# Batch 0 of a fused attention and feed-forward kernel, laid out as 72 rows of eight tokens instead of 96 rows of six

## The chip, the cores and the metric

The kernel runs on one NeuronCore of a Trainium2 chip. Its time is the device time of one launch in microseconds (us), and lower is better. The core has five engines that run side by side and meet through semaphores: TensorE (PE, matrix products; PEld is its weight load), VectorE (DVE), ScalarE (ACT), GpSimd (POOL) and SyncE (SP), which here only issues DMAs. Sixteen DMA engines move data between HBM and the on-chip memory SBUF, which has 128 partitions; a tile of R rows lies in R partitions. PSUM is the small memory that TensorE writes its results into.

## What is computed

```python
# q, k, v: (8, 8, 576, 64)   p: (8, 8, 32, 64)    batch, heads, tokens, width
p_packed = sm_attn(p, k, v)               # softmax over the 576 tokens
out      = sm_attn(q, p_packed, p_packed) # softmax over the 32 packed rows
x = out.transpose(0, 2, 1, 3).reshape(8 * 576, 512)
h = x @ w_in                              # w_in: 512 x 2048, float64
g = h * tanh(softplus(h))                 # "mish"
return (g @ w_out).astype(float32)        # w_out: 2048 x 512, float64
```

## The kernel before

**Two kinds of work.** Nearly all of the time goes to the feed-forward products of the eight batches, 16 steps of 128 hidden columns per batch (`t` counts them over all batches). Each step does an "up" product into `ps_h`, `mish` on ACT, and a "down" product into four accumulators `acc`. The attention of batch b+1 is woven between the steps of batch b. Only the attention of batch 0 has nothing to hide behind: it is the opening, written out by hand line by line, and the engines SP, DVE, ACT and POOL follow that written order up to the end of batch 0. TensorE follows the written order throughout.

**The opening.** Heads are taken in two groups g = 0, 1 of four. `load_heads` fetches one group of k, q or v in two DMAs of two heads each, 288 KB a DMA, into tiles `[R, 2, NI, 2*D]`. With `SI = 6` tokens to a row there are `R = 96` rows, and one contiguous run of HBM is 6 x 64 x 4 = 1536 bytes; `NI = SI // 2 = 3`. The tiles k_t, q_t and v_t share one tag with `KVB = 8` buffers, so the loads of the second group of q and of v wait until TensorE has read k_t. The steps are, for each g:

- `turn_keys` and `turn`: 4 transposes for each of the `NI` slices, then one copy per slice from PSUM (`ps_kq`) to `kT` or `qT`, on the engines named in the call.
- `score`, `spread`, `sums`: the first scores, their exponentials into the tile `a1` (`a` in the profile), the sums.
- `turn_weights`: the exponentials are transposed into PSUM and copied to `a1T`.
- `values`: 4 x `SI` small products of `a1T` with `v_t`, summed over the `SI` tokens of a row in PSUM (`ps_pp`), then scaled into `pp`. `turn_values` transposes that into `ppT`.
- `match`, `peak`, `rise`, `tally`, `divide`, `back`: the second scores, which DVE transposes into `a2`, their softmax, and the result `at` that the feed-forward steps read. `a2` has the tag `"a"` with one buffer, which it shares with `a1`: DVE can only write `a2` when TensorE has read the last of `a1` in `turn_weights(1)`.
- `warm(n)`: n products on zeros, which keep TensorE running.

**The weights** arrive as float64 and are turned into float32 on the chip, in 32 pieces of 512 KB. `fetch(n)` issues the DMAs of the pieces up to n into `w_st` (`STB = 8` buffers), `words(n)` does the two ACT passes (L591, L592) and the two POOL passes (L593, L597) of the pieces up to n, and `join(n)` the two DVE passes (L603, L608). The pieces are here called w0, w1 and so on: w0, w1, w3, w4, w7, w8 are of w_in (2 KB runs), w2, w5, w6 of w_out (4 KB runs). `w_out` piece i is needed by the down product of step i. The loop calls `join(2t + 5)` and `words(2t + 9)` in the steps t up to 13, and `join(3)` in step 0.

**The DMA queue.** All loads go out on SP in written order. The tool that builds the program gives the DMAs eight semaphores in turn, so that a DMA is issued only after the eighth before it has landed.

**The end of batch 0.** `rows(c)` cuts the 128 rows of chunk c of the output into pieces that lie in one token position each, one DMA for each piece: eight DMAs in batch 0.

Of the kernel before, what the change touches and what calls it, by code (L numbers as in the profile page):

```python
# [8 lines left out]
F32 = mybir.dt.float32  # L9
F32R = mybir.dt.float32r  # L10
# [5 lines left out]

LAG = 2
GB = 3
KVB = 8
KQB = 5  # L20
STB = 8
WB = 4
# [17 lines left out]
def body(  # L40
# [12 lines left out]
    B, H, S, D = q.shape  # L53
    NP = p.shape[2]
    DF = w_in.shape[1]
    DO = w_out.shape[1]
    P = 128
    SI = 6
    R = S // SI
    NI = SI // 2  # L60
    NX = 9
# [10 lines left out]
    att = ctx.enter_context(tc.tile_pool(name="att", bufs=2))  # L72
    stat = ctx.enter_context(tc.tile_pool(name="stat", bufs=2))
    wts = ctx.enter_context(tc.tile_pool(name="wts", bufs=2))
    moe = ctx.enter_context(tc.tile_pool(name="moe", bufs=2))
    ps_acc = ctx.enter_context(tc.tile_pool(name="ps_acc", bufs=4, space=bass.MemoryType.PSUM))
    ps_h = ctx.enter_context(tc.tile_pool(name="ps_h", bufs=2, space=bass.MemoryType.PSUM))
    ps_a = ctx.enter_context(tc.tile_pool(name="ps_a", bufs=2, space=bass.MemoryType.PSUM))
# [40 lines left out]
    w_out_v = w_out.bitcast(I32).rearrange("(t p) m -> p t m", p=P)  # L119
    out_v = out.rearrange("(b p si) m -> b si p m", p=R, si=SI)  # L120

    def load_heads(src, b, g, tag):
        ts = []
        for h0 in (4 * g, 4 * g + 2):
            t = early.tile([R, 2, NI, 2 * D], F32, name=tag, tag="kvq", bufs=KVB)
            nc.sync.dma_start(
                out=t, in_=src[b, h0:h0 + 2].rearrange("h (p i x) d -> p h i (x d)", i=NI, x=2)
            )
            ts.append(t)
        return ts  # L130

    def of_slot(ts, g, h):


        return ts[h // 2][:, (h % 2) ^ g]

    def psum(pool, shape, name):
        return pool.tile(shape, F32, name=name, tag="acc" if pool is ps_acc else "ps_a")
# [31 lines left out]
    class Batch:  # L170
# [11 lines left out]

        def start(self, pool):
            self.ppT = moe.tile([P, 2, P], F32, name="ppT")
            self.aT_hi = moe.tile([P, 2, S], F32R, name="aT_hi")
            self.aT_lo = moe.tile([P, 2, S], F32R, name="aT_lo")
            self.qT, self.a1T, self.pp, self.floats = {}, {}, {}, {}
            self.pT = att.tile([P, 2, P], F32, name="pT", bufs=1)
            self.a1 = att.tile([P, 2, 2, NI, R], F32, name="a1", tag="a", bufs=1)
            self.rs = stat.tile([P, 2], F32, name="rs")  # L190
            ps = psum(pool, [P, 2, P], "ps_p")
            for g in range(2):
                nc.tensor.transpose(
                    out=ps[:, g, :], in_=self.p_t[:, g].rearrange("a u d -> a (u d)"), identity=ident
                )
            nc.vector.tensor_copy(out=self.pT[:, 0], in_=ps[:, 0])
            pairs = [x.rearrange("p (m t n) -> p m t n", t=2, n=NP) for x in (self.pT[:, 1], ps[:, 1])]
            for t in range(2):
                nc.vector.tensor_copy(out=pairs[0][:, :, t], in_=pairs[1][:, :, 1 - t])
# [40 lines left out]
        def values(self, g, pool):  # L240
            pp_ps = psum(pool, [P, D], "ps_pp")
            for n in range(SI):
                i, u = n // 2, n % 2
                for h in range(4):
# [3 lines left out]
                        rhs=of_slot(self.v_t[g], g, h)[:, i, u * D:(u + 1) * D],  # L248
                        start=(n == 0), stop=(n == SI - 1),
                        tile_position=(0, h * NP),  # L250
# [25 lines left out]
        def match(self, g, pool):  # L276

            s2 = scores(pool, self.ppT[:, g, :], self.qT[g])
            if g == 0:
                self.a2 = att.tile([P, 2, S // NP, NP], F32, name="a2", tag="a", bufs=1)  # L280
            a2f = self.a2[:, g].rearrange("a g n -> a (g n)")
            for u in range(2):
                nc.vector.transpose(out=a2f[:, u * HALF:(u + 1) * HALF], in_=s2[u])
            yield
# [78 lines left out]
        def rest_rows(self):  # L363
            return out_v[self.b, SI - 1, R - REST:R, :]

# [3 lines left out]
    class Later(Batch):  # L369
# [38 lines left out]

        def start(self):
            self.ppT = moe.tile([P, 2, P], F32, name="ppT")  # L410
            self.aT_hi = moe.tile([P, 2, S], F32R, name="aT_hi")
            self.aT_lo = moe.tile([P, 2, S], F32R, name="aT_lo")
            self.pp, self.floats = {}, {}
            self.pT = att.tile([P, 2, P], F32, name="pT", bufs=1)
            self.a1 = att.tile([P, 2, NX, NP, 2], F32, name="a1", tag="a", bufs=1)
            self.rs = stat.tile([P, 2], F32, name="rs")
            self.pinned(nc.vector.transpose(
                out=self.pT.rearrange("a g n -> a (g n)"), in_=self.p_t.rearrange("a h d -> a (h d)")
            ))
# [153 lines left out]
    class Weight:  # L573
# [6 lines left out]
        def fetch(self):  # L580
            self.st = stg.tile([P, 2 * FC], I32, name="w_st")
            nc.sync.dma_start(
                out=self.st.rearrange("p (m x) -> p m x", m=2),
                in_=w_in_v[:, 2 * self.g:2 * self.g + 2, self.n * FC:(self.n + 1) * FC],
            )
            self.dst = wi[self.n // 2][self.g][:, self.n % 2].rearrange("p m x -> p (m x)")

        def words(self):
            x = self.st.rearrange("p (n t) -> p n t", t=2)
            self.r = stg.tile([P, FC], I32, name="wround", bufs=WB)  # L590
            nc.scalar.activation(out=self.dst, in_=x[:, :, 1].bitcast(F32), func=AF.Copy, scale=F64_SCALE)  # L591
            nc.scalar.activation(out=self.r, in_=x[:, :, 0].bitcast(U32), func=AF.Copy, scale=2.0 ** -29)  # L592
            nc.gpsimd.tensor_scalar(  # L593
                out=self.dst, in0=self.dst, scalar1=F64_HIGH, scalar2=-F64_HIGH, op0=ALU.min, op1=ALU.max
            )
            self.sign = stg.tile([P, FC], F32, name="wsign", bufs=WB)
            nc.gpsimd.tensor_scalar(  # L597
                out=self.sign, in0=self.dst, scalar1=0.0, scalar2=1.0, op0=ALU.mult, op1=ALU.mult
            )

        def join(self):
            bits = self.dst.bitcast(I32)
            nc.vector.scalar_tensor_tensor(  # L603
                out=bits, in0=bits, scalar=3, in1=self.sign.bitcast(I32),
                op0=ALU.logical_shift_left, op1=ALU.bitwise_or,
            )
            yield
            nc.vector.tensor_tensor(out=bits, in0=bits, in1=self.r, op=ALU.add)  # L608
# [28 lines left out]
    def packed_floats(n, g):  # L637
        if g == 0:
            whole[n] = wts.tile([P, 2, QC], F32, name="wp_0", tag="wp_hi", bufs=4)
        ps = ps_a.tile([P, QC], F32, name=f"ps_w{g}", tag="ps_a")  # L640
        for h in range(4):
            weave(0, ps, wi[n // 2][g][:, n % 2, h // 2], g, h)
        nc.scalar.copy(out=whole[n][:, g], in_=ps)
        return whole[n]
# [144 lines left out]
    def together(*gens):  # L789
        gens = list(gens)  # L790
        while gens:
            gens = [x for x in gens if next(x, "end") != "end"]
# [30 lines left out]
    def warm(n):  # L823
        for _ in range(n):
            nc.tensor.matmul(out=ps_warm, lhsT=still, rhs=still, start=True, stop=True)  # L825
# [28 lines left out]
    with tc.manual_schedule(engines={mybir.EngineType.PE}):  # L854
        first = batches[0]
# [7 lines left out]
        first.k_t.append(load_heads(k, 0, 1, "k_t"))  # L863
        fetch(1)
        first.q_t = [load_heads(q, 0, 0, "q_t")]
        first.v_t = [load_heads(v, 0, 0, "v_t")]
        first.start(ps_a)
        first.turn_keys(0, ("ACT", "DVE", "ACT"))
        first.q_t.append(load_heads(q, 0, 1, "q_t"))
        fetch(2)  # L870
        warm(WARM[1])
        first.score(0)
        first.turn_keys(1, ("ACT", "DVE", "ACT"))
        first.spread(0)
        first.v_t.append(load_heads(v, 0, 1, "v_t"))
        fetch(STB)
        words(1)
        first.sums(0)
        warm(WARM[1])
        first.score(1)  # L880
        together(first.turn_weights(0, ps_acc, ("DVE", "ACT")))
        first.spread(1)
        together(first.turn(0, ps_acc, ("ACT", "ACT", "ACT")))
        join(1)
        first.sums(1)
        together(first.values(0, ps_a))
        warm(WARM[2])
        together(first.turn_values(0, ps_a))
        words(2)
        warm(WARM[2])  # L890
        together(first.match(0, ps_acc))
        together(first.turn_weights(1, ps_acc, ("ACT", "ACT")))
        first.peak(slice(0, 1))
        together(first.turn(1, ps_acc, ("ACT", "ACT", "ACT")))
        first.rise(slice(0, 1))
        together(first.values(1, ps_a))
        warm(WARM[2])
        join(2)
        together(first.turn_values(1, ps_a))
        first.tally(slice(0, 1))  # L900
        words(3)
        warm(WARM[2])
        together(first.match(1, ps_acc))
        first.peak(slice(1, 2))
        first.rise(slice(1, 2))
        first.divide(slice(0, 1))
        first.back(0)
        packed_floats(0, 0)
        wps = {(0, 0): packed_floats(0, 1)}
        words(4)  # L910
        nc.scalar.preload_act_table_set("mish")
        warm(WARM[3])
        first.tally(slice(1, 2))
        first.back(1, 2)
        words(5)
        groups = []
        gen = iter(())
        g_rest = None
# [120 lines left out]
```

## Time and profile before

| | us |
|---|---|
| median of 3 runs (lowest, highest) | 751.86 (750.21, 754.09) |
| the profiled execution's own time | 754.06 |
| its span in the profile | 752.1 |
| granted TensorE clock, mean | 0.997 |
| PE busy | 735.8 (98%) |
| DVE, ACT, POOL busy | 423.3, 298.3, 53.1 |

The profile shows one execution. A window view gives the busy time of each engine in a stretch of time, which for PE is close to the whole stretch except at the beginning. A timeline row has start, duration, engine, line, operation and tiles; in square brackets stands how long the engine was idle before it and what ended that. In the view of the DMA queues "us to landing" is the time from the issue of a DMA until all of it has arrived, and the share of a queue is the time that its packets took, out of the time of 16 engines.

### The profile page before, as it was taken

The page shows a single profiled execution, that of the slowest core. Times are in us where ns is not written, and L with a number is a line of the kernel's source. Part 1 is how long each engine was busy: PE and PEld are TensorE (multiplying, and loading weights), DVE is VectorE, ACT ScalarE, POOL GpSimd, SP SyncE. Part 2 cuts the span into 40 slices and gives each one's busy share as a digit, 9 for nine tenths or more (in the row PEclk, how much of TensorE's full clock was granted, in tenths as well). Part 3 has the DMA queues.
Part 4 walks back from the last instruction along what each step waited for, and adds up shares of the span by engine and source line. Part 5 has one row for each costly group of instructions (what it writes and reads, how often), then busy time and mean ns, then how long its engine had stood idle before and what let it go on. Part 6 is the DMA issues. An engine that isn't in the chain of part 4 may idle for free.

```text
span 752.1 us, 12729 instructions
## 1 busy us (share of the span) xinstructions
PE 735.8 (98%) x5162; PEld 565.4 (75%) x5162; DVE 423.3 (56%) x723; ACT 298.3 (40%) x696; POOL 53.1 (7%) x70
## 2 busy tenths in 40 slices
PE   9789999999999999999999999999999999999997
PEld 7545554678787888877788878877888777888886
DVE  3789767765846456464834547373753637332332
ACT  4675755453532524252522524243433424232221
POOL 1285440000000000000000000000000000000000
PEclk9999999999999999999999999999999999999999
DMA  9999970554204450143302442052201100010002
GB/s 229 286 283 228 297 131 1 118 80 88 39 1 103 67 99 1 56 72 64 64 1 71 71 96 32 10 111 40 57 1 42 29 2 1 1 57 1 0 1 71
DMA packets 186874, 56.40 MB, mean 75 GB/s; under 512 B 173760, under 2 KB 176064, under 8 KB 186816
## 3 DMA queue, kind: packets, MB, share of 16 engines
q1 hardware_dynamic: 186816, 55.59, 31.9%
q8 instruction: 41, 0.67, 0.4%
q14 instruction: 17, 0.14, 0.1%
HBM read 46.14 MB, written 9.44 MB: 74 GB/s over the span
## 4 chain that ended last, share of the span: by engine, by line
PE 91%; DVE 3%; ACT 3%; DMA 1%; issue 1%; POOL 0%; SPq 0%; POOLq 0%; ACTq 0%
PE ps_h L704 25%; PE acc L741 15%; PE acc L743 14%; PE acc L742 14%; PE acc L761 5%; PE ps_w L622 4%; PE ps_s L437 3%; PE ps_rest L743 2%; PE ps_rest L742 2%; PE ps_rest L741 2%; PE ps_pp L492 2%; DMA w_st<-in_moe_w_in_dram 1%; PE ps_warm L825 1%; PE ps_a L479 1%; PE ps_h L716 1%
## 5 line engine op out<-in xcount | busy, mean ns | idle before, releaser
L725 ACT ACTIVATE g<-ps_h 128x288 f32<-128x288 f32 (+1 forms) x256 | 97.8, 385 | 315.3 <-PE ps_h L704 282.8
L741 PE MATMUL acc<-wo_hi,g_hi 128*128 128x512 f32 x448 | 183.4, 409 | 0.0
L743 PE MATMUL acc<-wo_hi,g_lo 128*128 128x512 f32 x448 | 176.5, 394 | 0.0
L742 PE MATMUL acc<-wo_lo,g_hi 128*128 128x512 f32 x448 | 176.3, 394 | 0.0
L704 PE MATMUL ps_h<-aT_hi,wp_hi 128*128 128x288 f32 x496 | 157.5, 318 | 0.7 <-ACT g L725 0.7
L704 PE MATMUL ps_h<-aT_lo,wp_hi 128*128 128x288 f32 x496 | 146.1, 295 | 0.0
L704 PE MATMUL ps_h<-aT_hi,wp_lo 128*128 128x288 f32 x496 | 145.7, 294 | 0.0
L736 DVE CAST g_hi<-g 128x512 fp32r<-128x512 f32 x112 | 47.6, 425 | 163.2 <-ACT g L725 163.0
L741 PEld LDWEIGHTS acc<-wo_hi,g_hi 128*128 128x128 f32 x448 | 84.0, 187 | 43.2 <-issue 27.8
L704 PEld LDWEIGHTS ps_h<-aT_hi,wp_hi 128*128 128x128 f32 x496 | 93.1, 188 | 16.2 <-issue 3.8
L704 PEld LDWEIGHTS ps_h<-aT_lo,wp_hi 128*128 128x128 f32 x496 | 93.2, 188 | 14.7 <-issue 5.5
L743 PEld LDWEIGHTS acc<-wo_hi,g_lo 128*128 128x128 f32 x448 | 84.1, 188 | 19.7
L704 PEld LDWEIGHTS ps_h<-aT_hi,wp_lo 128*128 128x128 f32 x496 | 93.1, 188 | 0.0
L742 PEld LDWEIGHTS acc<-wo_lo,g_hi 128*128 128x128 f32 x448 | 84.3, 188 | 8.7
L737 DVE TENSOR_TENSOR g_lo<-g,g_hi 128x512 fp32r<-128x512 f32 x112 | 77.3, 690 | 5.8
L761 PE MATMUL acc<-wo,g 128*128 128x512 f32 x128 | 64.3, 606 | 3.3 <-DVE wo L608 1.6
L634 DVE TENSOR_TENSOR wp_lo<-ps_w,wp_hi 128x512 fp32r<-128x512 f32 x56 | 36.1, 684 | 16.7 <-ACT wp_hi L633 16.7
L633 ACT CAST wp_hi<-ps_w 128x512 fp32r<-128x512 f32 x56 | 30.1, 590 | 31.0 <-PE ps_w L622 31.0
L622 PE MATMUL ps_w<-wi,ppT 64*32 64x512 f32 (+1 forms) x576 | 38.1, 553 | 0.2 <-DVE wi L608 0.2
L761 PEld LDWEIGHTS acc<-wo,g 128*128 128x128 f32 x128 | 21.3, 189 | 21.8 <-issue 11.7
L727 ACT ACTIVATE g_rest<-ps_h 128x64 f32<-128x64 f32 x128 | 28.1, 220 | 0.0
L743 PE MATMUL ps_rest<-wo_hi,r_lo 128*128 128x512 f32 x64 | 25.1, 393 | 0.0
(113 smaller groups left out, 741.6 us busy)
## 6 DMA issues: line engine op xcount, KB each, us to landing
w_st<-in_moe_w_in_dram SPq DMA_DIRECT2D x16, 512.0 KB, 7.7
w_st<-in_moe_w_out_dram SPq DMA_DIRECT2D x16, 512.0 KB, 7.2
k_n<-in_k_dram SPq DMA_DIRECT2D x56, 144.0 KB, 3.2
q_n<-in_q_dram SPq DMA_DIRECT2D x56, 144.0 KB, 3.2
v_n<-in_v_dram SPq DMA_DIRECT2D x56, 128.0 KB, 2.7
out_dram<-o SPq DMA_DIRECT2D x28, 256.0 KB, 2.0
k_t<-in_k_dram SPq DMA_DIRECT2D x4, 288.0 KB, 4.3
q_t<-in_q_dram SPq DMA_DIRECT2D x4, 288.0 KB, 8.5
```

The lines of the kernel that those rows point to most:

```text
L622: nc.tensor.matmul(out=ps[h * NP:(h + 1) * NP, :], lhsT=ppTb[row:row + D, g, h * NP:(h + 1) * NP], rhs=w[row:row + D], start=True, stop=Tr ...
L633: nc.scalar.copy(out=hi, in_=ps)
L634: nc.vector.tensor_tensor(out=lo, in0=ps, in1=hi.bitcast(F32), op=ALU.subtract)
L704: nc.tensor.matmul(out=ps, lhsT=w[:, fs], rhs=a[:, g, cs], start=(n == 0), stop=(n == 5))
L725: nc.scalar.activation(out=self.act[:, hf * HALF:hf * HALF + m], in_=ps[:, :m], func=AF.Mish)
L727: nc.scalar.activation(out=self.g_rest[self.b % 2][self.f // 4][:, self.f % 4, :], in_=ps[:, m:], func=AF.Mish)
L736: nc.vector.tensor_copy(out=hi, in_=self.act)
L737: nc.vector.tensor_tensor(out=lo, in0=self.act, in1=hi.bitcast(F32), op=ALU.subtract)
L741: nc.tensor.matmul(out=acc, lhsT=hi[:, cs], rhs=wh, start=start, stop=False)
L742: nc.tensor.matmul(out=acc, lhsT=hi[:, cs], rhs=wl, start=False, stop=False)
L743: nc.tensor.matmul(out=acc, lhsT=lo[:, cs], rhs=wh, start=False, stop=stop)
L761: nc.tensor.matmul(out=accs[c], lhsT=grp.act[:, cs], rhs=wo[f], start=f == 0, stop=f == NF - 1)
```

## The change

Batch 0 is laid out with `SI = 8`, so `R = 72`, `NI = 4`, and a contiguous run is 2048 bytes; the tiles grow by a third per partition and `KVB` falls from 8 to 6, so that v waits for k's buffers. The loads and the weight steps are written in another order: w1 is fetched ahead of v, w2 and w3 ahead of the second group of v, and the ACT and DVE passes of several pieces move to earlier places. `a2` is put into a spare buffer of the tag of `aT_hi`.

```diff
-KVB = 8
+KVB = 6
-    SI = 6
+    SI = 8
-            self.aT_hi = moe.tile([P, 2, S], F32R, name="aT_hi")
+            self.aT_hi = moe.tile([P, 2, S], F32R, name="aT_hi", tag="aT_hi")
...
-                self.a2 = att.tile([P, 2, S // NP, NP], F32, name="a2", tag="a", bufs=1)
+                self.a2 = moe.tile([P, 2, S // NP, NP], F32, name="a2", tag="aT_hi")
...
         first.k_t.append(load_heads(k, 0, 1, "k_t"))
         fetch(1)
         first.q_t = [load_heads(q, 0, 0, "q_t")]
+        fetch(2)
+        first.start(ps_a)
+        first.turn_keys(0, ("ACT", "DVE", "ACT", "DVE"))
         first.v_t = [load_heads(v, 0, 0, "v_t")]
-        first.start(ps_a)
-        first.turn_keys(0, ("ACT", "DVE", "ACT"))
-        first.q_t.append(load_heads(q, 0, 1, "q_t"))
-        fetch(2)
         warm(WARM[1])
         first.score(0)
-        first.turn_keys(1, ("ACT", "DVE", "ACT"))
+        first.turn_keys(1, ("ACT", "DVE", "ACT", "DVE"))
+        first.q_t.append(load_heads(q, 0, 1, "q_t"))
+        fetch(4)
         first.spread(0)
-        first.v_t.append(load_heads(v, 0, 1, "v_t"))
-        fetch(STB)
         words(1)
         first.sums(0)
         warm(WARM[1])
         first.score(1)
         together(first.turn_weights(0, ps_acc, ("DVE", "ACT")))
         first.spread(1)
-        together(first.turn(0, ps_acc, ("ACT", "ACT", "ACT")))
+        words(2)
+        together(first.turn(0, ps_acc, ("ACT",) * 4))
+        first.v_t.append(load_heads(v, 0, 1, "v_t"))
+        fetch(STB)
         join(1)
         first.sums(1)
         together(first.values(0, ps_a))
         warm(WARM[2])
         together(first.turn_values(0, ps_a))
-        words(2)
+        join(2)
         warm(WARM[2])
         together(first.match(0, ps_acc))
         together(first.turn_weights(1, ps_acc, ("ACT", "ACT")))
         first.peak(slice(0, 1))
-        together(first.turn(1, ps_acc, ("ACT", "ACT", "ACT")))
+        together(first.turn(1, ps_acc, ("ACT",) * 4))
         first.rise(slice(0, 1))
         together(first.values(1, ps_a))
         warm(WARM[2])
-        join(2)
         together(first.turn_values(1, ps_a))
         first.tally(slice(0, 1))
         words(3)
         warm(WARM[2])
         together(first.match(1, ps_acc))
         first.peak(slice(1, 2))
+        words(4)
         first.rise(slice(1, 2))
...
-        words(4)
         nc.scalar.preload_act_table_set("mish")
+        words(6)
         warm(WARM[3])
         first.tally(slice(1, 2))
         first.back(1, 2)
-        words(5)
```

More of the change, by code (lines that the diff above doesn't have):

```diff
@@ L410, in start @@
             self.ppT = moe.tile([P, 2, P], F32, name="ppT")
-            self.aT_hi = moe.tile([P, 2, S], F32R, name="aT_hi")
+            self.aT_hi = moe.tile([P, 2, S], F32R, name="aT_hi", tag="aT_hi")
             self.aT_lo = moe.tile([P, 2, S], F32R, name="aT_lo")
```

## Prediction

> **What bounds the kernel now.** I read the header first, then a window view of four stretches.
>
> ```profile
> span 752.1 us, 12729 instructions
> 0.00:20.00 20.00, 18.27 (x203) 15.38 (x203) 6.32 (x19) 8.41 (x21) 1.93 (x8) 1.00 0.95 227
> 20.00:45.00 25.00, 18.74 (x165) 12.10 (x165) 19.75 (x32) 18.36 (x38) 11.43 (x14) 0.93 1.00 309
> 45.00:150.00 105.00, 102.12 (x651) 59.29 (x650) 84.12 (x128) 61.28 (x136) 39.79 (x48) 1.00 0.67 164
> 150.00:750.00 600.00, 596.68 (x4147) 478.63 (x4145) 313.09 (x545) 210.21 (x503) 0.00 (x0) 1.00 0.21 45
> ```
>
> After the stretch, the columns are the busy time of PE, PEld, DVE, ACT and POOL, then the granted clock, the DMA share and GB/s. From 150 us on TensorE lacks 3.3 us of 600, and the change leaves that work alone. In 20 to 45 us it lacks 6.3 us of 25, and the DMA engines are busy all the time (0.95 and 1.00). So the end moves by as much as the beginning of the steady part, near 45 us, moves. The list of waits of the first 45 us and the chain of waits say what sets that.
>
> ```profile
> ACT wi L591 <- DMA w_st<-in_moe_w_in_dram: 2.7, 1, 2.7
> PE ps_kq L152 <- ACT a1T L144: 2.5, 1, 2.5
> PE acc L761 <- DVE wo L608: 1.6, 1, 1.6
> ```
>
> ```profile
> 10.00 10.95 DMA w_st<-in_moe_w_in_dram
> 20.95 0.02 issue
> 20.97 0.66 ACT wi L591
> 21.63 0.56 ACT wround L592
> 22.19 0.37 ACT a1T L144
> 22.56 0.04 issue
> 22.60 1.21 PE ps_kq L152 x12
> 23.81 1.37 PE ps_pp L245 x48
> ...
> 35.84 0.73 DVE wo L603
> ...
> 42.81 0.04 DVE wo L603
> 42.85 0.57 issue
> 43.42 1.11 DVE wo L608
> ```
>
> The chain begins with a DMA: w1 takes 10.95 us to arrive, ACT stands at words(2) until 20.97, the copy of `a1T` that stands behind it comes at 22.19, and TensorE idles 2.5 us. After that the chain is attention on TensorE and DVE up to 35.84, then the weight passes, and at their end TensorE waits 1.6 us for w5.
>
> **The change part by part.**
>
> *The stall on w1.* The copy of `a1T` could begin when TensorE has its input:
>
> ```profile
> 19.23 0.86 PE L236 MATMUL ps_a<-ident,a 128*96 128x128 f32 x6
> 20.12 0.85 DVE L283 STREAM_TRANSPOSE a<-ps_s 128x288 f32<-128x288 f32 x2 [3.06 <-PE ps_a L236]
> 23.24 1.24 ACT L144 COPY qT<-ps_kq 128x384 f32<-128x384 f32 x3 [0.32 <-PE ps_kq L152]
> 15.78 1.00 PE L245 MATMUL ps_pp<-v_t,a1T 96*32 96x64 f32 x48
> ```
>
> That is 20.1 instead of 22.1, so 2.0 us are at stake. Words(2) does not vanish, though: its 1.2 us of ACT (20.97 to 22.19) now stand ahead of the copies of qT(0), on the way to the first match. Net, 0.8 us could be won, if nothing else is late. The own buffer of `a2` lets DVE begin at the end of the scores, 0.9 us before 20.12 (TensorE went on to ps_a at 19.23); no piece of the chain above 22 us is DVE's work on g = 0, so nothing on the path.
>
> *What is late next: v.* The diff puts w1 ahead of v of g = 0, and w2 and w3 ahead of v of g = 1, which is moreover issued only when q's buffers are free. TensorE cannot do `values(1)` without the latter (the 23.81 row). When does it arrive?
>
> ```profile
> 11.57 1.13 SPq L126 DMA_DIRECT2D v_t<-in_v_dram  x2
> v_t<-in_v_dram SPq DMA_DIRECT2D x1, 288.0 KB, 10.9
> DMA packets 700, 1.00 MB, mean 249 GB/s; under 512 B 51, under 2 KB 700, under 8 KB 700
> DMA packets 553, 1.18 MB, mean 392 GB/s; under 512 B 36, under 2 KB 36, under 8 KB 553
> ```
>
> The second row is of the second of the two DMAs, issued within 12.2 to 13.0 us, about 12.4 by the rows' spacing; it lands at 12.4 + 10.9 = 23.3, half a microsecond before it is used. The third row is the stretch 11 to 15 us, in which only 96-row loads move (249 GB/s), the fourth 28 to 31 us, with 128-row weight loads (392 GB/s). The queue stays full, so a load lands when the bytes ahead of it have moved. Two weight pieces more ahead of v cost 524 KB / 392 GB/s = 1.34 us each, or 2.1 us at 249 GB/s: 2.7 to 4.2 us together; I take 3.4, since a piece between such loads meets both rates.
>
> *What a 72-row load costs.* Twelve of them stand ahead of the end of v. No 72-row load is in the trace. What it does have is the output of the same size, 256 KB in 2 KB runs, from 128 rows (583.5 to 585.5 us) and from twice 64 rows (585.5 to 587.5 us):
>
> ```profile
> q1 hardware_dynamic: 144, 0.26, 34.3%
> q1 hardware_dynamic: 160, 0.26, 62.5%
> ```
>
> The packets of the same bytes took 34.3% against 62.5% of 16 engines x 2 us, so 11.0 us against 20.0 us: 382 GB/s with 128 rows, 210 GB/s with 64. With 249 GB/s for 96 rows, what counts is the number of partitions. Between 64 and 96 rows the straight line gives 220 GB/s at 72, so 295 KB take 1.34 us; if the rate goes with the rows, 249 x 72/96 = 187 GB/s and 1.58 us. Today it is 1.18 us. I take 1.45, the middle, as 64 rows are the nearer row and 96 rows the same kind of load. Twelve loads: 12 x 0.27 = 3.2 us (1.9 to 4.8). The ends beyond that are the first two rivals.
>
> The Trainium skill, "SBUF — State Buffer", section "Door 1: The DMA port swizzle", says that bandwidth goes with how many of 16 ports the partitions reach, and that partitions 0 to 63 share eight of them. An estimate from that: those eight carry 64/96 of a load's bytes now and 64/72 after, 1.33 times as many, so a load lasts 1.18 x 1.33 = 1.57 us, and the sum below would be 1.4 us higher. The two output rows agree with it.
>
> *So v arrives at* 23.3 + 3.4 + 3.2 = 29.9 (27.9 to 32.3), and `values(1)` starts 6.1 us later than 23.8. It then replaces everything before it: v of g = 0 lands some 9 us earlier (four 72-row loads and two pieces), at about 20.7, against 15.78 now, and from `values(0)` to `values(1)` it is 8.0 us now, 2.0 of them the w1 stall: attention would be ready at 26.7. The late q, the wait of ACT for w1 ahead of qT(0), and the 16 transposes for 12 lie under that cover of 3 us; the four copies of 288 columns for three of 384 cost some 0.1 us of ACT a turn (1.24 us for three) there too. If the cover went, they would cost 0.1 to 0.5 us.
>
> *Values.* 64 products for 48: 1.37 / 48 x 16 = 0.46 us, behind the wait, on the path.
>
> *Weight steps.* From `match(1)` on the order is the same but for ACT. Words(4) goes into an idle time:
>
> ```profile
> 31.00 0.68 ACT L298 ACTIVATE a<-a 128x576 f32<-128x576 f32 x1 [2.55 <-DVE a L292]
> 34.66 0.67 ACT L591 ACTIVATE wi<-w_st 128x512 f32<-128x512 f32 x1
> 39.16 0.69 ACT L591 ACTIVATE wo<-w_st 128x512 f32<-128x512 f32 x1
> 40.96 1.12 POOL L593 TENSOR_SCALAR wo<-wo 128x512 f32<-128x512 f32 x1
> 42.81 0.69 DVE L603 SCALAR_TENSOR_TENSOR wo<-wo,wsign 128x512 int32<-128x512 int32 x1 [1.21 <-POOL wsign L597]
> 44.57 1.12 PE L761 MATMUL acc<-wo,g 128*128 128x512 f32 x2 [1.57 <-DVE wo L608]
> ```
>
> Its 1.1 us fit into 2.55; words(6) puts w5 where 34.66 has w4. So w6's ACT pass moves from 39.16 to where w5's was, 1.1 us earlier, POOL follows with w5's 2 us already done, and DVE (L603 at 42.81, behind POOL by 1.21) gets the sign some 1.8 us earlier. TensorE's 1.57 us at 44.57 go: -1.6. Late next is DVE itself, and w7 and later ones, which land after v and before their passes; if w5 were late, the 1.57 would stay.
>
> *Batch 0's output* has 2 + 3 + 3 + 3 pieces instead of 8: three more issues on SP of 0.4 to 0.6 us, at the end of batch 0. Behind them stand loads for batch 2 with tens of microseconds to spare. Batch 1's `aT_hi` waits for `a2`'s buffer, free since 36 us. Both nothing.
>
> *Sum.* 6.1 + 0.46 - 1.6 = +5.0 us (3.0 to 7.4 with the ends above). The profiled execution took 754.06, its span 752.1; it is 2.2 above the median. Its 754.06 becomes 759.1, and the median 751.86 becomes **756.8** (754.8 to 759.3).
>
> **The rivals.**
>
> *Long runs are what counts (not slower).* The weights' 2 KB runs move at 392 GB/s and the 1.5 KB runs at 249; if the run decides, a 72-row load takes 0.75 us, v lands at 23.3 + 2.7 - 12 x 0.43 = 20.8 and waits for nobody. Then 0.8 of the w1 stall and 1.6 of the weights are won and 0.46 lost: -1.9, 750.0. It decides as soon as a load takes under about 1.0 us. For it: no row has 1.5 KB runs on 128 partitions. Against it: 2 KB runs from 64 rows moved at 210.
>
> *Bytes count (same).* The load keeps 249 GB/s and 1.18 us; v lands at 26.7, +2.9 + 0.46 - 1.6 = +1.8, 753.6. For it: the rate is flat in 11 to 15 us. Against it: the output rows.
>
> *Fewer DMA engines.* If 72 rows are dealt to twelve engines, at the present 249 / 16 = 15.6 GB/s each, that is 187 GB/s and 1.58 us: v at 23.3 + 3.4 + 4.8 = 31.5, +6.6, 758.4. No run here shows a load on fewer than 16 engines. The Trainium skill, "DMA: Bandwidth & Descriptors", section "Why a DMA increments its semaphore by 16 and not by 1", has such a rule: the largest number up to 16 that divides the outer size, 16 for 96 and 12 for 72.
>
> **How the numbers follow.** Forecast 0.47, long runs 0.16, bytes 0.20, fewer engines 0.17. Half a per cent, 3.8 us, is about what a measurement of this kernel can tell from no change; that is 748.1 and 755.6. Of the forecast's own range (754.8 to 759.3) four fifths lie above 755.6, with nearly all of the fewer engines: slower 0.53. Faster by that much needs the long runs and also the clock dip (0.93 in 20 to 45 us) gone: 0.07. The range from 750.5 to 760.0 leaves out half of the first rival and the upper tails.
>
> **What would show it.** In the profile after: TensorE idle ahead of L245 until about 30 us with v_t as the last to land, where ACT's 2.7 us for w_st is gone or has moved ahead of the second group; q and v loads at 190 to 220 GB/s in the stretch where only they move; the DVE pass on w2 (L603, 35.84 now) near 42.4; no wait of L761 for L608 near 49 us; the stretch after 150 us unchanged. Wrong would be: v_t landing under 25 us, more than 249 GB/s in those loads, or a new wait on a weight pass after `match(1)`.

## The result, and the profile after

The changed kernel takes 756.91 us (median of 11 executions, 753.74 to 759.93), the kernel before 750.88 (11 executions, 749.74 to 754.09): ratio 1.0069, 95% interval 1.0045 to 1.0092, so 0.7% slower. Measured once more, on another occasion, it was 755.75 against 752.47, ratio 1.0044 (1.0023 to 1.0065).

The two profiled executions show almost none of that: the one after took 753.74 us, the fastest of its eleven, the one before 754.06, next to the slowest of its eleven (754.09). So the profile after is read for where it waits, and further executions for how much that costs.

The window view of the kernel after, in the stretches shown before:

```profile
0.00:20.00 20.00, 15.68 (x200) 13.68 (x201) 8.38 (x23) 9.25 (x23) 3.16 (x10) 0.94 0.87 234
20.00:45.00 25.00, 22.59 (x221) 15.75 (x220) 18.01 (x30) 17.13 (x38) 10.07 (x12) 0.84 0.99 302
45.00:150.00 105.00, 102.10 (x650) 59.17 (x650) 84.29 (x128) 61.31 (x136) 39.96 (x49) 1.00 0.67 164
150.00:750.00 600.00, 596.76 (x4148) 478.81 (x4146) 313.11 (x545) 210.17 (x503) 0.00 (x0) 1.00 0.21 45
```

From 45 us on nothing has changed. TensorE's idle time has moved from the second stretch into the first, and the granted clock fell, from 1.00 and 0.93 to 0.94 and 0.84. The list of waits of the first 45 us:

```profile
PE ps_pp L245 <- DMA v_t<-in_v_dram: 2.8, 2, 1.8
PE acc L761 <- DVE wo L608: 0.5, 1, 0.5
```

ACT's 2.7 us behind w1 are gone, TensorE's 1.6 us for w5 are 0.5, and a new wait stands at the head of TensorE's: 2.8 us for v. The chain of waits:

```profile
8.30 9.32 DMA v_t<-in_v_dram
...
17.66 1.88 PE ps_pp L245 x60
...
22.61 1.14 PE ps_s L161 x16
...
26.35 1.03 PE ps_pp L245 x64
...
44.75 1.13 PE acc L761 x2
```

The DMA that the chain begins with is now v of g = 0. The two rows after it are slow: `match(0)` (L161) takes 1.14 us where `match(1)` before took 0.66. A window view of the kernel after says why:

```profile
17.00:25.00 8.00, 7.34 (x97) 5.91 (x98) 2.54 (x5) 1.15 (x4) 0.00 (x0) 0.57 1.04 303
25.00:34.00 9.00, 7.31 (x145) 6.13 (x143) 6.56 (x12) 7.30 (x17) 3.05 (x4) 1.00 0.93 305
```

The granted clock is 0.57 over the 8 us after the wait and 1.00 in the next nine. Loads of v landed, by the completion events in the trace, at 17.61 (first group) and 25.94 us (second group), against 15.88 and 23.29 in the kernel before.

One number serves to compare executions below: the start of the down product on w5 (the row of L761 that waits for L608), 44.57 us before and 44.75 after. From there to the end of the span it is 707.2 to 707.5 us in every kernel below but one (e12), so the opening alone decides.

### The profile page after: what moved, and what is told of

It is laid out like the page before. It is cut to its first block, busy times and chain, and to the rows that moved or that the text cites. A ratio compares the mean times of both kernels' runs of the same rounds, so it can differ in the third digit from the quotient of the medians.

```text
span 752.0 us, 12843 instructions
## 1 busy us (share of the span) xinstructions
PE 737.1 (98%) x5214; PEld 567.4 (75%) x5214; DVE 423.8 (56%) x725; ACT 297.9 (40%) x698; POOL 53.2 (7%) x70
## 4 chain that ended last, share of the span: by engine, by line
PE 90%; ACT 3%; DVE 2%; DMA 2%; issue 1%; POOL 0%; SPq 0%; ACTq 0%; DVEq 0%; POOLq 0%
PE ps_h L704 25%; PE acc L741 15%; PE acc L743 14%; PE acc L742 13%; PE acc L761 5%; PE ps_w L622 4%; PE ps_s L437 3%; PE ps_rest L743 2%; PE ps_rest L742 2%; PE ps_rest L741 2%; PE ps_pp L492 2%; PE ps_warm L825 1%; DMA v_t<-in_v_dram 1%; PE ps_a L479 1%; DMA out_dram<-o 1%
## 5 line engine op out<-in xcount | busy, mean ns | idle before, releaser
L761 PE MATMUL acc<-wo,g 128*128 128x512 f32 x128 | 64.2, 606 | 2.2 <-ACT g L725 1.5
L761 PEld LDWEIGHTS acc<-wo,g 128*128 128x128 f32 x128 | 21.4, 189 | 20.4 <-issue 11.7
L742 PE MATMUL ps_rest<-wo_lo,r_hi 128*128 128x512 f32 x64 | 25.1, 393 | 0.0
```

The lines of the kernel that those rows point to most:

```text
L742: nc.tensor.matmul(out=acc, lhsT=hi[:, cs], rhs=wl, start=False, stop=False)
L761: nc.tensor.matmul(out=accs[c], lhsT=grp.act[:, cs], rhs=wo[f], start=f == 0, stop=f == NF - 1)
```

## The experiments

**The changed kernel again** (e1), no edit.

> The changed kernel once more, to see another of its executions (753.74 to 759.93 us so far, and the profiled one was the fastest). Theory A: the executions differ in the opening, before 45 us: v of g = 0 lands after TensorE has asked for it, TensorE idles, and its clock is halved for stretches of 3.4 us at a time, whose place differs from execution to execution. Then a slower execution shows TensorE steady 2 to 6 us later than the 44.75 of the profiled one, and the same time from there to the end. Rival B: the executions differ after 45 us, with the opening unchanged. Median 756 to 758.

755.75 us (753.15 to 759.26), ratio to before 1.0044 (1.0023 to 1.0065). Its profiled execution took 755.81. The timeline of TensorE:

```profile
15.62 0.30 PE L245 MATMUL ps_pp<-v_t,a1T 72*32 72x64 f32 x4 [1.15 <-DMA v_t<-in_v_dram]
18.39 1.92 PE L245 MATMUL ps_pp<-v_t,a1T 72*32 72x64 f32 x60 [2.47 <-DMA v_t<-in_v_dram]
27.71 1.09 PE L245 MATMUL ps_pp<-v_t,a1T 72*32 72x64 f32 x60 [0.79 <-DMA v_t<-in_v_dram]
46.80 1.12 PE L761 MATMUL acc<-wo,g 128*128 128x512 f32 x2 [0.50 <-DVE wo L608]
```

Steady 2.05 us later than the 44.75, and span 754.0 against 752.0: theory A, though the median lies just under the expected 756 to 758. Both groups of v are waited for; they land at 18.34 and 27.67.

**Layout and order apart** (e2, e3).

```diff
# e2, from the changed kernel
-KVB = 6
+KVB = 8
-    SI = 8
+    SI = 6
# e3, from the kernel before
-KVB = 8
+KVB = 6
-    SI = 6
+    SI = 8
...
-("ACT", "DVE", "ACT")            # twice
+("ACT", "DVE", "ACT", "DVE")
-("ACT", "ACT", "ACT")            # twice
+("ACT",) * 4
```

> The changed kernel with 96 rows of six tokens and eight buffers again, its order of loads and weight steps and its own buffer for a2 kept. Theory A (the 72-row loads take 1.40 us instead of 1.19 and so v is late): v of both groups lands some 2 us earlier than in the changed kernel, 749.5 to 752. Rival C (the order, w1 ahead of v, w2 and w3 ahead of the second v, is what costs): no better than 755.

> The kernel before with 72 rows of eight tokens and six buffers alone, its order of loads and weight steps kept. Theory A: every q, k and v load costs 0.2 us more and v of g = 0 waits for k's buffers, so 753 to 757. Rival C: the layout alone costs nothing, 750 to 752.

e2: 754.82 us, ratio 1.0022 (1.0004 to 1.0041). e3: 756.43 us, ratio 1.0042 (1.0022 to 1.0062). Each half costs time alone. Together they gave 1.0044 in the same comparison; with these intervals that is not told apart from the sum of the two. e2 lies between its two ranges, close to rival C, and e3 where theory A put it. In e2 v is late without 72 rows, in e3 the old wait behind w1 has stayed, TensorE does not wait for v, and the clock is low behind the wait (`values(1)` takes 1.94 us):

```profile
16.59 0.86 PE L245 MATMUL ps_pp<-v_t,a1T 96*32 96x64 f32 x44 [0.71 <-DMA v_t<-in_v_dram]
25.30 1.50 PE L245 MATMUL ps_pp<-v_t,a1T 96*32 96x64 f32 x44 [0.79 <-DMA v_t<-in_v_dram]
46.57 1.12 PE L761 MATMUL acc<-wo,g 128*128 128x512 f32 x2 [0.49 <-DVE wo L608]
```

```profile
23.75 1.95 PE L152 MATMUL ps_kq<-ident,q_t 72*128 72x72 f32 x16 [1.58 <-ACT a1T L144]
25.63 1.94 PE L245 MATMUL ps_pp<-v_t,a1T 72*32 72x64 f32 x64
47.48 1.13 PE L761 MATMUL acc<-wo,g 128*128 128x512 f32 x2 [1.57 <-DVE wo L608]
```

**The late weight steps alone** (e4), from the kernel before.

```diff
+        words(4)
         first.rise(slice(1, 2))
...
-        words(4)
         nc.scalar.preload_act_table_set("mish")
+        words(6)
...
-        words(5)
```

> The kernel before with only the late weight steps moved on ACT: words(4) ahead of the second exponentials and words(6) after the table load. The prediction's step: TensorE's wait of 1.57 us for w5 goes, 749.0 to 749.8. Rival D: something else is late at that place and nothing is won, 750.5 to 751.5.

752.05 against 752.47, ratio 0.9990 (0.9970 to 1.0010): above both ranges, and the time cannot tell e4 from the kernel before. The trace can. TensorE's 1.57 us for w5 fell to 0.49, but two waits for w3 and w4 took part of it:

```profile
39.20 0.64 PE L622 MATMUL ps_w<-wi,ppT 64*32 64x256 f32 x8 [0.59 <-DVE wi L608]
40.21 0.64 PE L622 MATMUL ps_w<-wi,ppT 64*32 64x256 f32 x8 [0.38 <-DVE wi L608]
43.26 1.13 PE L761 MATMUL acc<-wo,g 128*128 128x512 f32 x2 [0.49 <-DVE wo L608]
```

From the first up product (31.79) to the down product on w5 it is 11.47 us; in e8 below, with the old steps, 11.98. So the steps are worth about 0.5 us here (0.8 by the same count in e10 below), not 1.6: DVE's passes are next.

**TensorE kept busy in the first wait** (e5), from the changed kernel.

```diff
+        warm(8)
         together(first.values(0, ps_a))
```

> The changed kernel with eight more products on zeros ahead of values(0), where TensorE waits for v of g = 0 (2.8 us in the profiled execution, 3.6 in the second one, after which the granted clock was 0.50 for 6.8 us). Theory A (the idle stretch takes the clock down, and the half clock then stretches values(0), the warm products and the first match): the clock stays at 1.00 from 17 to 25 us and TensorE is steady 1.5 to 3 us earlier, 752.5 to 754.5. Rival: the clock has no part in it, or another wait ends last, so 755 to 757.

758.21 us (6 executions, 755.01 to 759.09), ratio 1.0065 (1.0046 to 1.0085): the rival, 1.2 us above its range. The clock did hold from 17 to 25 us, but the time went into the next wait, behind which the clock fell after all (0.73 from 25 to 30 us):

```profile
17.62 1.10 PE L245 MATMUL ps_pp<-v_t,a1T 72*32 72x64 f32 x64
24.51 0.30 PE L245 MATMUL ps_pp<-v_t,a1T 72*32 72x64 f32 x4 [1.30 <-DMA v_t<-in_v_dram]
25.89 1.09 PE L245 MATMUL ps_pp<-v_t,a1T 72*32 72x64 f32 x60 [1.08 <-DMA v_t<-in_v_dram]
46.45 1.12 PE L761 MATMUL acc<-wo,g 128*128 128x512 f32 x2 [0.50 <-DVE wo L608]
```

`values(0)` takes 1.10 us for all 64 products instead of 1.88 for sixty (the profile counts each product in float32 twice: the eight on zeros stand there as x16). TensorE asks for the second v at 23.2 and gets it at 25.89. In the changed kernel `values(1)` starts at 26.28, so the half clock there had only hidden this wait.

**v ahead of w1** (e6), from the kernel before, with e4's steps.

```diff
         first.q_t.append(load_heads(q, 0, 1, "q_t"))
-        fetch(2)
...
-        words(2)
...
         together(first.values(1, ps_a))
+        words(2)
         warm(WARM[2])
-        join(2)
         together(first.turn_values(1, ps_a))
         first.tally(slice(0, 1))
+        join(2)
         words(3)
```

> The kernel before, with the opposite order: the second v ahead of w1, w1's passes after values(1), and the late weight steps as in the change. If the opening is bound by what the DMA queue brings first (theory A), the wait of ACT for w1 goes, values(1) starts about 2 us earlier than in the kernel before (some 15.8 us after the first warm products end, now), and the time is 749.5 to 751 where the kernel before takes 752. Rival: DVE's pass on w1 now stands ahead of the second match and takes that back, 752.

751.87 against 752.81, ratio 0.9985 (0.9971 to 0.9999): the rival's time. `values(1)` starts at 20.70, 13.4 us after the first warm products end, and no longer waits behind w1. Part of that went as the rival said: the join of w1 now holds up DVE and the next products.

```profile
26.57 0.64 PE L622 MATMUL ps_w<-wi,ppT 64*32 64x256 f32 x8 [1.27 <-DVE wi L608]
30.62 2.87 PE L716 MATMUL ps_h<-at,wp 128*128 128x288 f32 x10 [1.21 <-DVE at L330]
```

The down product on w5 starts at 42.10, later than in e10 below (40.83, the old order). The granted clock was 1.00 in all 45 us of e6's opening, where the kernel before had 0.93 from 20 to 45 us, so the small gain may be the clock's alone.

**Partitions or DMA engines** (e7), from the changed kernel.

```diff
-            nc.sync.dma_start(out=t, in_=rows)
+            nc.sync.dma_start(out=t[:64], in_=rows[:64])
+            nc.sync.dma_start(out=t[64:], in_=rows[64:])
```

> The changed kernel with each load of q, k and v cut into rows 0 to 63 and rows 64 to 71, two DMAs. If the partitions decide (forecast), the 64 rows alone take about as long as the 72 did, 1.3 to 1.5 us for both, and the time is that of the changed kernel or up to 2 us more. If the twelve engines decide (rival), 64 rows go over sixteen and a load takes 1.05 to 1.2 us, v lands 1 to 3 us earlier, 752 to 754.

761.03 us, ratio 1.0105 (1.0087 to 1.0123), 2 to 3 us above what was expected. The completion events in the trace number 12 for a 72-row load, besides one right behind its issue, and 16 for a weight piece, so a 72-row load does run on twelve engines, and 64 rows on sixteen. That brought no speed: the two loads of a pair, each of 64 and 8 rows, landed 1.46 us apart as a median of six pairs, against 1.33 in the profile of the changed kernel. The queue of e7 from 13 to 18 us, with its packets above:

```profile
DMA packets 544, 1.02 MB, mean 203 GB/s; under 512 B 55, under 2 KB 55, under 8 KB 543
q1 hardware_dynamic: 543, 1.00, 106.8%
```

Sixteen engines, busy all the time, move 203 GB/s, in loads of 64 and 8 rows and parts of w0 and w1. So it is the number of partitions that limits the load, as in the prediction's output rows (210 GB/s from 64 rows). The Trainium skill ("SBUF — State Buffer", "Door 1: The DMA port swizzle"), by which the first 64 partitions share eight ports, agrees with that. That the second v came 6.3 us later than in the changed kernel (32.26) is not the loads' doing: w0 to w3 took 11.5 us of the time between landings instead of 5.9. Why is not shown. A DMA is issued only when the eighth before it has landed, and there are twice as many; SP stood 2.2 and 2.8 us at an issue until w0 and w1 had landed.

**The wait filled in the kernel before** (e8).

```diff
         first.peak(slice(0, 1))
+        warm(6)
         together(first.turn(1, ps_acc, ("ACT", "ACT", "ACT")))
```

> The kernel before with six more products on zeros ahead of the second turn, in TensorE's wait of 2.5 us behind w1. Theory A (idle TensorE loses its clock): no stretch of 0.50 between 21 and 30 us, 0.5 to 1.5 us less than the kernel before. Rival: no difference.

751.17 us (750.68 to 752.58) against 752.81 (749.74 to 755.52), ratio 0.9980 (0.9968 to 0.9993). The window view of e8:

```profile
20.00:45.00 25.00, 20.13 (x180) 12.73 (x179) 20.85 (x34) 20.17 (x42) 13.49 (x17) 1.00 1.01 307
```

The clock stays at 1.00 where the kernel before had 0.93, the median falls by 1.6 us, and the spread is a third: theory A, and a little more than was expected.

**All four combinations with filled waits** (e9 to e12): the same edit as in e5 and e8, `warm(n)` ahead of the steps that wait. e9 is the changed kernel with 8 and 10 ahead of `values(0)` and `values(1)`; e10 the kernel before with e8's fill and e4's steps; e11 is e3 with 6 ahead of `turn(1)` and 4 ahead of `values(1)`; e12 is e2 with 7 and 13 ahead of `values(0)` and `values(1)`.

> The changed kernel with products on zeros in both waits, eight ahead of values(0) and ten ahead of values(1), so that the clock has no reason to dip. Theory A in its present form (the arrival of v, near 26 us, is the bound, and clock dips come on top): no stretch at 0.50, values(1) when v has landed, TensorE steady some 2.5 us later than in the kernel before with its own wait filled (751.2), so 753 to 754.5, and a narrower spread than the changed kernel's 753 to 760. Rival B (the dips are all of the loss): 751 to 752.

> The kernel before with its wait filled and the late weight steps moved. The moved steps are worth 1.1 us after the first up products (11.98 against 11.47 us from the first of these to the down product on w5 at an equal clock, and the wait of 1.57 falls to 0.5): 749.7 to 750.5. Rival D: no less than the filled kernel alone, 751.2.

> The kernel before with 72 rows and six buffers, its wait behind w1 and the one for the second v filled. Theory A: w1 lands at about 22 and the second v at about 25.4 instead of 22.5 to 23.4, so values(1) starts about 2.4 us later than with 96 rows, and 16 products more: 753.5 to 754.5. Rival (in the old order the layout costs nothing once the clock holds): 751 to 752.

> The new order with 96 rows and eight buffers, both waits for v filled (seven and thirteen products). Theory A: the second v still lands behind w2 and w3, at 24 to 25.4, which costs 1 to 2 us against the old order, less the 1.1 of the weight steps: 751 to 752.5. Rival (the order is free with 96 rows): 750 or less.

| | us (range) | ratio to before | first v, second v landed | `values(1)` in full from | down product on w5 |
|---|---|---|---|---|---|
| e8, 96 rows, old order | 751.17 (750.68 to 752.58) | 0.9980 (0.9968 to 0.9993) | 15.35, 22.32 | 22.93 | 42.28 |
| e10, the same, late weight steps | 750.60 (749.76 to 752.13) | 0.9983 (0.9967 to 0.9999) | 13.61, 20.35 | 21.84 | 40.83 |
| e11, 72 rows, old order | 754.92 (752.12 to 760.08) | 1.0042 (1.0019 to 1.0066) | 16.15, 23.23 | 24.28 | 43.75 |
| e12, 96 rows, new order | 756.21 (754.76 to 758.24) | 1.0059 (1.0037 to 1.0080) | 16.27, 26.11 | 26.15 | 45.02 |
| e9, 72 rows, new order | 756.18 (753.39 to 758.02) | 1.0052 (1.0030 to 1.0073) | 19.79, 28.97 | 29.19 | 47.65 |

e9 falls outside what was expected, 2 us above: in its profiled execution the second v landed at 28.97, not near 26, and `values(1)` followed at once.

```profile
19.83 1.09 PE L245 MATMUL ps_pp<-v_t,a1T 72*32 72x64 f32 x60 [1.14 <-DMA v_t<-in_v_dram]
29.19 1.10 PE L245 MATMUL ps_pp<-v_t,a1T 72*32 72x64 f32 x64
```

Nor did the clock hold. The window from 20 to 45 us in e9, e10 and e12:

```profile
20.00:45.00 25.00, 23.12 (x296) 17.82 (x288) 16.20 (x28) 14.75 (x32) 7.35 (x10) 0.86 0.99 277
20.00:45.00 25.00, 21.63 (x185) 13.44 (x184) 23.90 (x36) 18.97 (x39) 15.29 (x18) 1.00 0.96 289
20.00:45.00 25.00, 20.86 (x211) 13.99 (x195) 18.90 (x30) 16.96 (x36) 11.45 (x14) 1.00 0.97 290
```

So e9 does not show a loss without a fall of the clock. e12 against e10 does, for the order: both have 96 rows and the late weight steps, the clock is 1.00 in both openings, and the down product on w5 starts 4.2 us later with the new order, at the end of a chain that begins with the second v (below). These are single executions, and the second v alone landed anywhere from 20.35 to 23.29 in four traces of the old order with 96 rows (before, e4, e8, e10), so the size is rough.

e10 beats both kernels by a little (its interval reaches 0.9999), but is not better than e8: the ratios are 0.9983 and 0.9980. Its moved steps show only in the trace, 11.20 us from the first up product to the down product on w5 against 11.98 in e8. e11 is 0.4 us above its expected range, though its profiled execution (752.91) is below it; in that one the filler itself is on the path, since v had landed at 23.23. The chains of waits of e11 and of e12:

```profile
12.27 8.12 DMA w_st<-in_moe_w_in_dram
...
22.18 1.22 PE ps_kq L152 x16
23.41 0.94 PE ps_warm L825 x8
24.35 1.03 PE ps_pp L245 x64
```

```profile
14.13 11.98 DMA v_t<-in_v_dram
26.15 0.86 PE ps_pp L245 x44
```

e12's expectation was wrong by more: its profile shows the second v a little later than expected (26.11), and its remainder after the opening is 1.6 to 2.0 us longer than in the others. Two waits of 1.2 us in all, which e9 lacks, are part of it; the longer one:

```profile
497.52 1.51 PE L622 MATMUL ps_w<-wi,ppT 64*32 64x512 f32 x16 [0.89 <-DVE a L457]
```

Where they come from is not shown, so not all of e12's 756.21 is the order's.

## Why the prediction was right, and where it was not

**Right: what is late next.** The stall on w1 went and the wait for v took its place. e2 shows it for the order, and e5 (up to 25 us) and e12 show that it stays when the clock is held up. For the layout alone only the time shows a loss (e3, e11): there the chain still began with w1, and TensorE did not wait for the second v.

**Wrong: which v.** "It then replaces everything before it" gave 3 us of cover to the first v. In the profiled execution and in e1 the first v stands in the chain with idle times of 2.8 and 3.6 us, and the second is in time (26.28 against 25.94) or 0.79 us late. The second became the bound where the first wait was filled (e5). The cover failed on both its ends. The second v landed earlier than the forecast 29.9, and from `values(0)` to the end of the second turn it took 8.6 us in the profiled execution, at half the clock for most of it, not the 6.0 of the forecast; at a full clock (e5) it took 5.6.

**The 72-row load: right in mechanism and size.** Forecast 1.45 us for today's 1.18. The two loads of a pair landed, as a median of the six pairs, 1.33 us apart in the profile after, 1.41 in e3, e5 and e11, 1.46 in e1 and 1.64 in e9; with 96 rows 1.05 to 1.20. The prediction's estimate of 1.57 was too high for five of these six. The rival of long runs is refuted by all of them, and the twelve engines of the other rival exist but are not the limit (e7).

**The second v's landing: right to about 1 us, from a base that was late.** 29.9 was forecast; 25.94, 27.67, 25.85 and 28.97 came (after, e1, e5, e9), 27.1 as a mean. The base of 23.3 was the latest of four: with 96 rows and the old order of loads it was 23.29, 20.65, 22.32 and 20.35 (before, e4, e8, e10), 21.7 as a mean. Mean to mean that is +5.5 where +6.6 was forecast. The first two profiles alone give only +2.65, since one is the latest of its kind and the other among the earliest. The terms, as means of four traces against four:

- the eight loads from q of g = 0 on: 11.7 against 9.0 us, +2.7; forecast 2.16;
- the loads up to the last of k: 9.1 against 8.4, +0.7; forecast 1.08;
- w2 and w3: 3.1; forecast 3.4;
- w0 and w1, which the forecast left as they were: 3.2 together instead of 4.2, so -1.0. In the profile after, four of the sixteen shares of w1 had landed by 10.33 and the other twelve came from 14.26 on (before: all from 18.13 to 20.95). Four of the sixteen engines have no part in a 72-row load and carry their part of the weights in that time.

**Values: half the size.** 0.46 was taken from a row at a lowered clock. At 1.00, 64 products take 1.10 us (e5) and 48 take 0.88 (e8): 0.22.

**Weight steps: a third to a half.** 0.5 (e4) or 0.8 (e10 against e8) instead of 1.6, since the waits for w3 and w4 came in.

**Left out: the clock.** The forecast gave the dip a part in one rival only. TensorE waits were followed by stretches of 3.4 to 6.8 us at 0.50 in the profiles before, after, e1, e2, e3 and e4, and filling the wait of the kernel before took 1.6 us off its median (e8). The mean granted clock of every execution is on record. Of 80 executions of the kernel before, the 34 with 0.998 or more have a median of 750.65 us and the 20 below 0.996 one of 754.66. Of 23 of the changed kernel, the five with 0.998 or more have 754.65 and the 17 below 0.996 have 757.22. At a like clock the change costs 2.6 to 4.0 us, then, and the changed kernel also loses its clock more often. The executions were sorted, the clock was not set, so how much of the loss the clock causes stays open.

**The sum.** 756.8 and 756.91 agree better than their terms, and that is luck: the landing was forecast too late by 0.9 to 4.0 us, the weight steps too good by 0.8 to 1.1, and the clock and the first v were missing. The loss against the base was 6.0 us in one comparison and 3.3 in the other, so +5.0 is right within what these can tell.

**Open:** why the same loads take 1.33 us in one execution and 1.64 in another. The second v, which the changed kernel waits for, lands anywhere from 25.9 to 29, and that may be part of why its times spread over 6 us; no run sets it apart from the clock.

## What to carry to other kernels

In an opening that is bound by one DMA queue, moving a load forward delays all that it passes: look up which of these is used next, and how much slack its landing has (0.5 us in the profile before, 1.3 in e4), before removing a wait. Cost a load by the partitions it fills as well as by its bytes and run length. And keep TensorE busy through a wait that cannot be removed; here that, without any reordering, gave 0.2% (e8), while in the changed kernel it won nothing (e5, e9). Read more than one execution before sizing a term: the landing that this forecast started from differed by 3 us between four.

## What the runs showed of the hardware

A load of 72 rows ran on twelve DMA engines, one of 96, 128 or 64 rows on sixteen; yet sixteen engines moved only 203 GB/s in e7, in loads of 64 and 8 rows and parts of weight pieces, where loads of 128 rows alone had got 392. The engines that a 72-row load left out ran ahead with the next weight piece: four of its shares landed some 4 us before the other twelve. After waits of TensorE of 1.6 to 3.6 us, in one piece or two, the granted clock was 0.50 for one or two stretches of 3.4 us, which began 1.7 to 4.1 us after the idle time had (before, after, e1 to e5, e9). It does not always fall: idle stretches of 1.87 us in e10 and e12 were followed by none.
